# A fourth seven-product group in the gate and value half of a fused attention and SwiGLU kernel

## The chip, the cores and the metric

One core of a Trainium2 chip runs the whole kernel. The metric is the device time of one execution in microseconds (us). Every call of the chip ran the kernel before beside the kernels under test, on the same chip. A profile's span is shorter than the time by about 1.7 us.

The times of one kernel scatter by about 1% here. So, besides the times, I use the lengths of the nine chunks read from the traces.

## The reference, cut to what matters

```python
# attention over a window of 32 to both sides; q, k, v: 8 x 8 heads x 576 x 64
attn = softmax(scale * q @ k.T, masked to |i - j| <= 32) @ v
x = attn.transpose(0, 2, 1, 3).reshape(4608, 512)
# SwiGLU block, d_ff = 1536
g   = x @ w_gate
out = (g * sigmoid(g) * (x @ w_val)) @ w_out
```

## The kernel before

The 4608 tokens are worked in nine chunks of 512, numbered 0 to 8 as in the code. Each has an FFN1 part (gate and value, silu, product h) and an FFN2 part (times w_out). Attention for the next batch is threaded between the products of FFN2. It works on pairs of 64-token blocks (36 pairs, numbered through): scores (q times k), exponential, mask, product with v, normalisation to x. The pairs that the h sums below speak of are something else, pairs of h's column blocks, 0 to 5. TensorE does everything in fp16.

FFN1 of a chunk is 12 column blocks of 128. Two of them can be done "plainly", a unit of 8 matmuls of 512 columns each, or together as a "group": a 2 x 2 block product in seven instead of eight products, each of 4 matmuls of 256 columns. The seven products use three PSUM tiles. X is added to again and again, and copied or read in between:

```python
"P1": product("X", wv(0), b11, True)      # then s1: ScalarE copies X
"P2": product("Y", wv(1), b21, True)      # then c11: val half 0 = Y + s1   (VectorE)
"P5": product("Z", s1, xs[0], True)       # then p5: ScalarE copies Z
"P6": product("X", s2, xs[1], False)      # then u2: ScalarE copies X
"P7": product("X", s3, xs[2], False)      # then c22: gate = X + p5         (VectorE)
"P3": product("Z", s4, b22, False)        # then c12: val half 1 = Z + u2
"P4": product("X", wg(1), xs[3], False)   # adds onto what c22 read; then sd: silu(X)
"hm": h = silu * val                      # VectorE
```

`xs` are four differences of x (GpSimd), `s1` to `s4` here are weight sums, made once. The order is written by hand. `pg`, `pv` are the halves of plain units, `s`, `m` their silu and product; `A` and `B` are sums of h that FFN2 needs, `A` on GpSimd, `B` on VectorE. `q`, `k` issue loads:

```
pg0 pv0 s0 m0 q0 k0 q1 t0
1P1 1s1 1P2 1P5 1c11 1p5 1P6 pg1 1u2 s1 k1 check t1 t2 1P7 1P3 1c22 pv1 1c12 1sc 1P4 m1 1sd t3
... (group 2)
3P1 3P2 3s1 3P5 As3 k3 3c11 3p5 3P6 2hm q4 k4 pg3 3u2 s3 3P7 3P3 3c22 pv3 3c12 3sc 3P4 m3 3sd
pg4 3hm pv4 s4 t6 Bs0 m4 flag pg5 Bs1 pv5 s5 m5 Bs2
```

FFN2 is seven products p1 to p7 of the same kind, 12 matmuls of 256 columns each, over the PSUM tiles x and y. The start:

```python
st["p1"](); st["s1"]()                 # x; ScalarE copies it
last = wino_sums(j, 5, 6)              # VectorE: the last h sums
for f in last[:2] + list(late) + last[2:]: f()
scores(0, ps_c); scores(1); scores(2); exp(0); exp(1); exp(2)
st["p2"](); st["c11"]()                # y; VectorE: the y sum reads it
masked(0); masked(1); masked(2)
st["p6"](); st["u2"]()                 # x again
st["p5"]()                             # overwrites y: must wait for c11
```

## Time and profile before

| | before |
|---|---|
| median of 3 runs | 320.4 us (320.32 to 322.25) |
| span of the profile | 319.1 us |
| busy: TensorE, VectorE, ScalarE, GpSimd | 96, 70, 61, 55% |
| from a chunk's first plain half (pg0) to p5 of its FFN2, chunks 2 to 8 | 24.65, 24.65, 24.65, 24.64, 24.91, 23.91, 23.95 us |

The prediction shows the lines behind this. One more view: the chain of waits, which is followed back from the last instruction, at each step to what released it. Here it is from the end of FFN1 to p5 in chunk 4, in order of time (start, length, what):

```profile
172.67 0.44 PE gX_ps L484 x4
173.11 3.45 PE gv_ps L553 x16
176.56 1.31 PE x_ps L622 x12
177.87 0.81 PE s_ps L312 x48
178.68 1.42 PE y_ps L622 x12
180.10 1.31 PE x_ps L622 x12
181.41 1.31 PE y_ps L622 x12
```

Only TensorE is in it. P4 of the third group, two plain units (16 matmuls), p1, the scores of three pairs, p2, p6, p5: each starts when the one before it has been issued, and nobody is waited for.

### The profile page before, as it was taken

Reading aid. Unit: us, or ns where it says so; the run is one execution under the profiler, and the core shown is the slowest. Engines: PE = TensorE matmul, PEld = TensorE weight load, DVE = VectorE, ACT = ScalarE, POOL = GpSimd, SP = SyncE. Lnnn points to the kernel's source line nnn. Section 1 sums busy time; section 2 is a strip of 40 time slices with the busy share of each in tenths; the row PEclk is TensorE's granted clock in tenths of the full one; section 3 lists DMA queues with packets and bytes.
Section 4 is the critical chain, followed back from the end, with each engine's and each line's share of the span. In section 5 each row is a group of like instructions: output and inputs, shape, how many; then the busy total and the mean of one; then the engine's idle time right before and its main releaser. Section 6 shows DMA issues by size and latency. Waiting matters only on the chain.

```text
span 319.1 us, 8056 instructions
## 1 busy us (share of the span) xinstructions
PE 306.0 (96%) x3180; PEld 210.3 (66%) x3180; DVE 222.3 (70%) x402; ACT 196.0 (61%) x309; POOL 175.5 (55%) x199
## 2 busy tenths in 40 slices
PE   6879999999999999999999999999999999999991
PEld 3444555575877587668766877677667766777581
DVE  3854498799866788668766886876578867737750
ACT  3874569664766576757566757584757576236530
POOL 8973678539359925885489239952530439004000
PEclk9999999999999999999999999999999999999997
DMA  7999999999959997999999999999553460030012
GB/s 280 176 195 302 236 173 187 199 131 159 147 149 130 147 157 163 126 152 157 190 110 160 153 157 155 155 166 166 138 112 77 99 89 0 24 109 2 0 52 89
DMA packets 157003, 44.46 MB, mean 139 GB/s; under 512 B 137504, under 2 KB 154400, under 8 KB 156960
## 3 DMA queue, kind: packets, MB, share of 16 engines
q0 software_dynamic: 100640, 16.52, 80.2%
q1 hardware_dynamic: 56320, 27.38, 43.6%
q8 instruction: 26, 0.43, 0.6%
q14 instruction: 17, 0.14, 0.2%
HBM read 37.75 MB, written 9.44 MB: 148 GB/s over the span
## 4 chain that ended last, share of the span: by engine, by line
PE 85%; DMA 6%; DVE 4%; ACT 2%; issue 1%; SPq 0%
PE gv_ps L553 26%; PE gX_ps L484 14%; PE x_ps L622 11%; PE y_ps L622 8%; PE gZ_ps L484 6%; PE gv_ps L427 6%; DMA xT<-x 3%; PE gY_ps L484 3%; PE ob L441 3%; PE o_ps L374 3%; PE s_ps L312 2%; DMA qk_st<-in_k_dram 2%; DVE p_t L358 1%; PE z_ps L622 1%; PE xt_ps L414 1%
## 5 line engine op out<-in xcount | busy, mean ns | idle before, releaser
L558 ACT ACTIVATE ssb<-gv_ps 128x512 f16<-128x512 f32 x48 | 28.7, 597 | 36.4 <-PE gv_ps L553 36.4
L553 PE MATMUL gv_ps<-xT,wg 128*128 128x512 f16 x192 | 49.3, 379 | 0.3 <-DMA xT<-x 0.2
L553 PE MATMUL gv_ps<-xT,wv 128*128 128x512 f16 x192 | 49.3, 379 | 0.0
L562 DVE TENSOR_TENSOR hT<-ssb,gv_ps 128x512 f16<-128x512 f16 x48 | 33.0, 687 | 20.3 <-ACT ssb L558 19.7
L542 POOL TENSOR_TENSOR x_sums<-xT 128x512 f16<-128x512 f16 x14 | 16.8, 1202 | 52.5 <-issue 26.6
L318 ACT ACTIVATE p_t<-s_ps 128x1024 f16<-128x1024 f32 (+1 forms) x40 | 34.6, 924 | 13.3 <-PE s_ps L312 13.3
L590 POOL TENSOR_TENSOR s_top<-hT 128x512 f16<-128x512 f16 x16 | 18.5, 1156 | 38.4 <-DVE hT L530 31.2
L484 PEld LDWEIGHTS <-g_top 128*128 128x128 f16 x288 | 26.8, 97 | 12.1 <-ACT kept L268 3.7
L622 PEld LDWEIGHTS <-hT 128*128 128x128 f16 x288 | 27.6, 98 | 5.1
L506 DVE TENSOR_TENSOR gate<-gX_ps,kept 128x512 f32<-128x512 f32 x24 | 16.6, 690 | 19.8 <-ACT kept L268 10.0
L553 PEld LDWEIGHTS <-wv 128*128 128x128 f16 x192 | 18.8, 98 | 17.5
L622 PEld LDWEIGHTS <-s_top 128*128 128x128 f16 x288 | 27.7, 98 | 3.5 <-issue 0.2
L268 ACT ACTIVATE kept<-gX_ps 128x512 f32<-128x512 f32 x48 | 28.6, 595 | 2.1 <-ACT kept L268 2.0
L484 PE MATMUL gX_ps<-x_sums,g_top 128*128 128x256 f16 x192 | 28.9, 272 | 0.1
L223 POOL DMA_DIRECT2D tok<-in_q_dram x30 | 26.0, 865 | 4.8 <-DMA qT<-tok 1.4
L553 PEld LDWEIGHTS <-wg 128*128 128x128 f16 x192 | 18.2, 98 | 14.3 <-issue 0.3
L223 POOL DMA_DIRECT2D tok<-in_k_dram x30 | 25.9, 863 | 0.6 <-DMA wo<-in_moe_w_out_dram 0.5
L392 DVE TENSOR_TENSOR x<-o_ps,rall 128x512 f16<-128x512 f32 x36 | 24.9, 691 | 1.2
L511 ACT ACTIVATE silu<-gate 128x512 f16<-128x512 f32 x24 | 15.1, 630 | 17.0 <-DVE gate L506 17.0
L622 PE MATMUL x_ps<-w_top,s_top 128*128 128x256 f16 x192 | 23.6, 273 | 0.0
L322 DVE TENSOR_TENSOR p_t<-p_t,mask 128x1024 f16<-128x1024 f16 x32 | 21.5, 706 | 2.0 <-ACT p_t L318 1.3
L242 POOL DMA_DIRECT2D v<-in_v_dram x24 | 21.5, 916 | 0.9 <-PE s_ps L312 0.9
(114 smaller groups left out, 610.2 us busy)
## 6 DMA issues: line engine op xcount, KB each, us to landing
out_dram<-osb SPq DMA_DIRECT2D x32, 256.0 KB, 3.1
v<-v SPq DMA_DIRECT2D x12, 264.0 KB, 6.4
v<-in_v_dram POOLq DMA_DIRECT2D x24, 128.0 KB, 7.8
tok<-in_q_dram POOLq DMA_DIRECT2D x24, 128.0 KB, 6.4
tok<-in_k_dram POOLq DMA_DIRECT2D x24, 128.0 KB, 6.9
qk_st<-in_q_dram SPq DMA_DIRECT2D x4, 576.0 KB, 7.0
qk_st<-in_k_dram SPq DMA_DIRECT2D x4, 576.0 KB, 10.1
v<-in_v_dram POOLq DMA_DIRECT2D x16, 96.0 KB, 6.9
```

Source lines behind the costliest of these rows:

```text
L223: nc.gpsimd.dma_start(out=t[0:n].rearrange("p (h d) -> p h d", d=D), in_=src[b].rearrange("h s d -> s h d")[128 * m:128 * m + n])
L242: nc.gpsimd.dma_start(out=dst[:, 2 * m, :, 0:D], in_=src[128 * m - 32:128 * m + 96])
L268: nc.scalar.activation(out=o, in_=i, func=AF.Copy, bias=0.0, scale=1.0)
L318: nc.scalar.activation(out=o, in_=s, func=AF.Exp, bias=0.0, scale=1.0 / float(D) ** 0.5)
L322: nc.vector.tensor_tensor(out=flat, in0=flat, in1=mask, op=ALU.mult)
L392: nc.vector.tensor_tensor(out=x16s[m][:, a], in0=ov[:, :, :, 0:D], in1=r.unsqueeze(3).to_broadcast([128, a.stop - a.start, 4, D]), op=ALU. ...
L427: nc.tensor.matmul(out=gv[:, i, :], lhsT=w[:, g, 128 * fk:128 * fk + 128], rhs=xts[j][:, g, :], start=(g == 0), stop=(g == GS - 1))
L484: nc.tensor.matmul(out=k[name][:, n], lhsT=lhs[:, g, 128 * n:128 * n + 128], rhs=rhs[:, g, :], start=(first and n == 0 and g == 0), stop=( ...
L553: nc.tensor.matmul(out=k["gv"][:, i, :], lhsT=w[:, g, 128 * fk:128 * fk + 128], rhs=xts[j][:, g, :], start=(g == 0), stop=(g == GS - 1))
L558: nc.scalar.activation(out=k["s"], in_=k["gv"][:, 0, :], func=AF.Silu, bias=0.0, scale=1.0)
L562: "m": lambda: nc.vector.tensor_tensor(out=hts[j][:, fk, :], in0=k["s"], in1=k["gv"][:, 1, :], op=ALU.mult)}
L622: nc.tensor.matmul(out=dst[n], lhsT=lhs[:, f, 128 * n:128 * n + 128], rhs=rhs[:, f, :], start=(first and f == 0 and (split or n == 0)), st ...
```

## The change

The intent: in chunks 2 to 8 a fourth group replaces two plain units, which takes matmul columns off the engine that is busy for 96% of the span. What else is in the change makes room for that:

```diff
-    xtpool = ...bufs=3                         # SBUF for four more weight sums
+    xtpool = ...bufs=2
+    gw["more"] = t1, t2, t3, t4                # made in chunk 0, from unit 7 on
+        "h1": lambda: hm(cols(0)),             # last group: h in two token halves
+        "h0": lambda: hm(cols(1)),
-                for f in range(FKS // 2):      # FFN2: pair 4, the last group, at the end
+                for f in (0, 1, 2, 3, 5, 4):
+    """, False: """                            # the order of chunks 2 to 8
+        pg0 1P1 1s1 1P5 1P2 1p5 1P6 1c11 1u2 q0 pv0 s0 k0 q1 1P7 1P3 1c22 pg1 1c12 1sc k1 1P4 m0 1sd check
...
+        4P1 4s1 4P2 4P5 q4 k4 3hm 4c11 4p5 4P6 Bs0 4u2 pv3 s3 4P7 4P3 4c22 sc0 sc1 4c12 4sc 4P4 4h0 m3 Bs1 Bs2
+        4sd 4h1
+    """}
-        for name, fs in (("A", wino_sums(j, 0, 2, nc.gpsimd)), ("B", wino_sums(j, 2, 5))):
+        for name, fs in (("A", wino_sums(j, 0, 2 if j == 1 else 1, nc.gpsimd)),
+                         ("D", wino_sums(j, 1, 2, nc.gpsimd)), ("B", wino_sums(j, 2, split))):
-        urgent = {1: (1, 2), 2: (1, 2), 3: (0, 1)}.get(j, ())
+        urgent = {1: (1, 2), 2: (1, 2), 3: (0, 1), 4: (1,), 5: (0,)}.get(j, ())
```

`sc0`, `sc1` are the scores of the first two attention pairs, moved up from behind p1. `urgent` names pairs whose x is turned (transposed) on TensorE instead of by DMA. The two token halves also change places in the groups, so that the half that FFN2 needs first is ready first. Chunk 1 keeps the old order, but has the two xT buffers and the changed order of halves and pairs too.

More of the change, by code (lines that the diff above doesn't have):

```diff
@@ L166 @@
     xpool = fast.enter_context(tc.tile_pool(name="xp", bufs=5))
-    xtpool = fast.enter_context(tc.tile_pool(name="xt", bufs=3))
+    xtpool = fast.enter_context(tc.tile_pool(name="xt", bufs=2))
     htpool = fast.enter_context(tc.tile_pool(name="ht", bufs=1))
@@ L463, in group_weights, with token_halves, group_steps @@
         t1, t2, t3, t4 = [t.rearrange("p k (a c) -> p k a c", c=256) for t in gw["s"]]
-        return [lambda k=k, o=o, a=a, b=b, op=op:
-                nc.vector.tensor_tensor(out=o[:, k], in0=a[:, k], in1=b[:, k], op=op)
-                for o, a, b, op in ((t1, g0, g1, ALU.add), (t2, t1, v0, ALU.subtract),
-                                    (t3, v0, g0, ALU.subtract), (t4, v1, t2, ALU.subtract))
-                for k in range(2)]
-    def group_steps(j, i, xs, tiles):
-        f = 2 * i
-        x = xts[j]
-        b11, b21, b22 = x[:, 0:2, 0:256], x[:, 2:4, 0:256], x[:, 2:4, 256:512]
-        wv = lambda k: wv16[:, 2 * k:2 * k + 2, 512 * i:512 * i + 256]
-        wg = lambda k: wg16[:, 2 * k:2 * k + 2, 512 * i:512 * i + 256]
-        s1, s2, s3, s4 = [t[:, :, 256 * i:256 * i + 256] for t in gw["s"]]
+        fs = [lambda k=k, o=o, a=a, b=b, op=op:
+              nc.vector.tensor_tensor(out=o[:, k], in0=a[:, k], in1=b[:, k], op=op)
+              for o, a, b, op in ((t1, g0, g1, ALU.add), (t2, t1, v0, ALU.subtract),
+                                  (t3, v0, g0, ALU.subtract), (t4, v1, t2, ALU.subtract))
+              for k in range(2)]
+        s5 = const.tile([128, 4, 2, 256], FP16, name="g_more")
+        gw["more"] = t1, t2, t3, t4 = [s5[:, n] for n in range(4)]
+        v0, v1, g0, g1 = [w[:, 2 * k:2 * k + 2, 768:1024] for w in (wv16, wg16) for k in range(2)]
+        return fs + [lambda o=o, a=a, b=b, op=op:
+                     nc.vector.tensor_tensor(out=o, in0=a, in1=b, op=op)
+                     for o, a, b, op in ((t1, g0, g1, ALU.add), (t2, t1, v0, ALU.subtract),
+                                         (t3, v0, g0, ALU.subtract), (t4, v1, t2, ALU.subtract))]
+    def token_halves(j):
+        x = xts[j]
+        return [x[:, 2 * k:2 * k + 2, 256 * c:256 * c + 256] for k in (0, 1) for c in (1, 0)]
+    def group_steps(j, f, xs, first, tiles):
+        b11, b12, b21, b22 = token_halves(j)
+        wv = lambda k: wv16[:, 2 * k:2 * k + 2, 256 * f:256 * f + 256]
+        wg = lambda k: wg16[:, 2 * k:2 * k + 2, 256 * f:256 * f + 256]
+        s1, s2, s3, s4 = (gw["more"] if f % 2 else
+                          [t[:, :, 128 * f:128 * f + 256] for t in gw["s"]])
         k = {}
-        first = "ZX" if i == 2 else "X"
+        cols = lambda c: slice(256 - 256 * c, 512 - 256 * c)
         def product(name, lhs, rhs, first):
@@ L500, in val @@
                 k["val"] = qk16.tile([128, 2, 512], FP16, tag="qk16", name="val")
-            nc.vector.tensor_tensor(out=k["val"][:, :, 256 * c:256 * c + 256], in0=k[src],
+            nc.vector.tensor_tensor(out=k["val"][:, :, cols(c)], in0=k[src],
                                     in1=k[name], op=ALU.add)
@@ L510, in silu, with hm @@
                 k["silu"] = qk16.tile([128, 2, 512], FP16, tag="qk16", name="silu")
-            nc.scalar.activation(out=k["silu"][:, :, 256 * c:256 * c + 256], in_=k[src],
+            nc.scalar.activation(out=k["silu"][:, :, cols(c)], in_=k[src],
                                  func=AF.Silu, bias=0.0, scale=1.0)
+        def hm(c):
+            nc.vector.tensor_tensor(out=hts[j][:, 2 * f:2 * f + 2, c], in0=k["silu"][:, :, c],
+                                    in1=k["val"][:, :, c], op=ALU.mult)
         return {
@@ L516, in group_steps @@
             "s1": lambda: keep_act("s1", "X"),
-            "P2": lambda: (bank("Y"), product("Y", wv(1), b21, True)),
+            "P2": lambda: ("Y" in k or bank("Y"), product("Y", wv(1), b21, True)),
             "c11": lambda: val(0, "Y", "s1"),
@@ L529, in group_steps @@
             "sd": lambda: silu(0, "X"),
-            "hm": lambda: nc.vector.tensor_tensor(out=hts[j][:, 2 * f:2 * f + 2, :],
-                                                  in0=k["silu"], in1=k["val"], op=ALU.mult),
+            "hm": lambda: hm(slice(0, 512)),
+            "h1": lambda: hm(cols(0)),
+            "h0": lambda: hm(cols(1)),
         }
     def x_sums(j, eng):
-        x = xts[j]
-        b11, b12 = x[:, 0:2, 0:256], x[:, 0:2, 256:512]
-        b21, b22 = x[:, 2:4, 0:256], x[:, 2:4, 256:512]
+        b11, b12, b21, b22 = token_halves(j)
         t = ppool.tile([128, 4, 2, 256], FP16, tag="p2", name="x_sums", bufs=2)
@@ L624, in product @@
                                      start=(first and f == 0 and (split or n == 0)),
-                                     stop=(f == FKS // 2 - 1), skip_group_check=True)
+                                     stop=(f == 4), skip_group_check=True)
         def keep_act(name, src):
@@ L765 @@
             tw = wino_weights()
-        if u >= 8:
-            if u == 8:
-                gsum = group_weights()
-            for f in gsum[2 * (u - 8):2 * (u - 8) + 2]:
-                f()
         if u == 4:
@@ L778 @@
             place_k(transpose_qk(c16[3]), 1, 1, cast_dve)
+        if u >= 7:
+            if u == 7:
+                gsum = group_weights()
+            for f in gsum[3 * (u - 7):3 * (u - 7) + 3]:
+                f()
     dummy = const.tile([1, 1], FP32)
@@ L812 @@
     carried = [8]
-    ORDER = """
+    ORDER = {True: """
         pg0 pv0 s0 m0 q0 k0 q1 t0
@@ L819, with ffn1_grouped @@
         pg4 3hm pv4 s4 t6 Bs0 m4 flag pg5 Bs1 pv5 s5 m5 Bs2
-    """
+    """, False: """
+        pg0 1P1 1s1 1P5 1P2 1p5 1P6 1c11 1u2 q0 pv0 s0 k0 q1 1P7 1P3 1c22 pg1 1c12 1sc k1 1P4 m0 1sd check
+        2P1 2s1 2P2 2P5 1hm As0 As1 q2 2c11 2p5 2P6 2u2 pv1 s1 As2 As3 k2 2P7 2P3 2c22 pg2 2c12 2sc 2P4 m1 2sd
+        3P1 3s1 3P2 3P5 2hm Ds0 Ds1 q3 3c11 3p5 3P6 3u2 pv2 s2 3P7 3P3 3c22 Ds2 Ds3 k3 pg3 3c12 3sc 3P4 m2 3sd flag
+        4P1 4s1 4P2 4P5 q4 k4 3hm 4c11 4p5 4P6 Bs0 4u2 pv3 s3 4P7 4P3 4c22 sc0 sc1 4c12 4sc 4P4 4h0 m3 Bs1 Bs2
+        4sd 4h1
+    """}
     def table(func):
         nc.scalar.activation(out=dummy, in_=rall[0:1, 0, 0:1], func=func, bias=0.0, scale=1.0)
-    def ffn1_grouped(j):
+    def ffn1_grouped(j, scores):
         b = j + 1
@@ L832, in ffn1_grouped @@
         carried.clear()
-        if pairs:
-            pair_av(pairs[0], ps_c, False)
-        if len(pairs) > 1:
-            pair_av(pairs[1], ps_a, False)
+        for n, m in enumerate(pairs):
+            pair_av(m, ps_c if j == 1 or n < len(pairs) - 1 else ps_a, False)
         for m in pairs:
@@ L847, in ffn1_grouped @@
             steps[f"t{i}"] = tw[i + 1] if j == 1 else lambda: None
-        banks = ({"X": ps_c, "Y": ps_o, "Z": ps_o}, {"X": ps_o, "Y": ps_c, "Z": ps_o},
-                 {"X": ps_o, "Y": ps_c, "Z": ps_o})
-        for i in range(3):
-            for name, f in group_steps(j, i, xs, banks[i]).items():
-                steps[f"{i + 1}{name}"] = f
-        for i, fk in enumerate((2, 3, 6, 7, 10, 11)):
+        if j == 1:
+            groups = ((0, "X", {"X": ps_c, "Y": ps_o, "Z": ps_o}),
+                      (2, "X", {"X": ps_o, "Y": ps_c, "Z": ps_o}),
+                      (4, "ZX", {"X": ps_o, "Y": ps_c, "Z": ps_o}))
+        else:
+            groups = [(f, first, {"X": ps_o, "Y": ps_c, "Z": ps_o})
+                      for f, first in ((0, "XZ"), (2, "ZX"), (3, "XZ"), (4, "ZX"))]
+        for i, (f, first, tiles) in enumerate(groups):
+            for name, fn in group_steps(j, f, xs, first, tiles).items():
+                steps[f"{i + 1}{name}"] = fn
+        for i, fk in enumerate((2, 3, 6, 7, 10, 11) if j == 1 else (2, 3, 10, 11)):
             for name, f in unit_steps(j, fk).items():
                 steps[f"{name}{i}"] = f
-        for name, fs in (("A", wino_sums(j, 0, 2, nc.gpsimd)), ("B", wino_sums(j, 2, 5))):
+        split = 5 if j == 1 else 4
+        for name, fs in (("A", wino_sums(j, 0, 2 if j == 1 else 1, nc.gpsimd)),
+                         ("D", wino_sums(j, 1, 2, nc.gpsimd)), ("B", wino_sums(j, 2, split))):
             for i, f in enumerate(fs):
                 steps[f"{name}s{i}"] = f
+        for i in range(2):
+            steps[f"sc{i}"] = scores[i] if i < len(scores) else lambda: None
         if j == NCH - 1:
@@ L869, in ffn1_grouped, with ffn2 @@
                 steps[f"{n}{m}"] = lambda m=m, n=n: load_qk(b + 1, (m,), n) if b + 1 < B else None
-        for name in ORDER.split():
+        for name in ORDER[j == 1].split():
             steps[name]()
-        return wino_sums(j, 2, 5)[3:]
-    def ffn2(j, todo, late=()):
-        st = wino_steps(j, j == NCH - 1)
+        return [wino_sums(j, 2, split)[3]] + wino_sums(j, split, 6)
+    def ffn2(j, todo):
         n = len(todo)
         ex = {}
-        urgent = {1: (1, 2), 2: (1, 2), 3: (0, 1)}.get(j, ())
+        urgent = {1: (1, 2), 2: (1, 2), 3: (0, 1), 4: (1,), 5: (0,)}.get(j, ())
         def scores(i, pool=None):
@@ L900, in norm @@
                     pair_xt(todo[i])
+        early = [lambda: scores(0, ps_c), lambda: scores(1)]
+        late, *last = ffn1_grouped(j, [] if j == 1 else early)
+        st = wino_steps(j, j == NCH - 1)
         if n:
@@ L905, in ffn2 @@
         st["s1"]()
-        last = wino_sums(j, 5, 6)
-        for f in last[:2] + list(late) + last[2:]:
-            f()
-        scores(0, ps_c)
-        scores(1)
+        for f in last[:2] + [late] + last[2:]:
+            f()
+        if j == 1:
+            for f in early:
+                f()
         scores(2)
@@ L948 @@
     for j in range(1, NCH):
-        late = ffn1_grouped(j)
-        ffn2(j, [m for m in range(NPAIR) if (2 * m + 1) // NT == j + 1], late)
+        ffn2(j, [m for m in range(NPAIR) if (2 * m + 1) // NT == j + 1])
     fast.close()
```

## The prediction

> **What bounds the kernel now.** I number the chunks as the code does, 0 to 8; the change touches 2 to 8 and leaves chunk 1 on the old order. In the text P1 to P7 are the seven products of an FFN1 group, X, Y, Z its three PSUM tiles; a plain unit is 8 matmuls of 512 columns; p1 to p7 are the seven products of FFN2, x and y its two PSUM tiles (y is used again as z); pg0 is the first plain half of a chunk. I read the page first, then the chain of waits in order of time, then the timelines of TensorE, VectorE and ScalarE through one chunk, and last the end of chunks 7 and 8.
>
> The page: engine totals, TensorE's row of the 40 slices, the chain by engine.
>
> ```profile
> PE 306.0 (96%) x3180; PEld 210.3 (66%) x3180; DVE 222.3 (70%) x402; ACT 196.0 (61%) x309; POOL 175.5 (55%) x199
> ...
> PE   6879999999999999999999999999999999999991
> ...
> PE 85%; DMA 6%; DVE 4%; ACT 2%; issue 1%; SPq 0%
> ```
>
> TensorE is never idle between slice 4 and the last one, so only two things can move the time: matmul work taken off it, and waits put onto it. Small waits do not show as idle there, because a row's duration includes the pipeline. They show as start-to-start distances. The timeline of TensorE in chunk 4, second group:
>
> ```profile
> 163.22 0.60 PE L484 MATMUL gX_ps<-xT,wv 128*128 128x256 f16 x4
> ...
> 164.57 0.60 PE L484 MATMUL gX_ps<-x_sums,g_top 128*128 128x256 f16 x4
> 165.00 1.03 PE L553 MATMUL gv_ps<-xT,wg 128*128 128x512 f16 x4
> 165.90 0.60 PE L484 MATMUL gX_ps<-x_sums,g_top 128*128 128x256 f16 x4
> ...
> 168.07 0.60 PE L484 MATMUL gX_ps<-xT,wv 128*128 128x256 f16 x4
> ```
>
> These rows are P1, P6, a plain half, P7 and the next group's P1. The chain of waits gives 0.87 us for 8 matmuls of 256 columns and 0.86 for 4 of 512, so 0.1088 and 0.2158 us each. Nominally a group with its two plain halves needs 28 x 0.1088 + 8 x 0.2158 = 4.77; it takes 168.07 - 163.22 = 4.85. The 0.08 are P6 waiting for the copy of X after P1 and P7 waiting for the copy after P6 (165.90 - 164.57 = 1.33 where 1.30 would do). So the groups already run at the limit of their copies.
>
> The end of FFN1 in chunk 7, on VectorE, then on TensorE:
>
> ```profile
> 274.60 0.69 DVE L562 TENSOR_TENSOR hT<-ssb,gv_ps 128x512 f16<-128x512 f16 x1 [0.63 <-ACT ssb L558]
> 275.20 0.75 DVE L590 TENSOR_TENSOR s_top<-hT 128x768 f16<-128x768 f16 x2
> ...
> 277.07 0.68 DVE L651 TENSOR_TENSOR osb<-y_ps,kept 128x512 f32<-128x512 f32 x1
> ```
> ```profile
> 276.33 1.47 PE L622 MATMUL x_ps<-w_top,s_top 128*128 128x256 f16 x12
> 277.81 1.47 PE L622 MATMUL y_ps<-w_top,s_top 128*128 128x256 f16 x12
> ```
>
> 277.81 is p5. It overwrites y, so it has to wait for the sum that reads y (277.07 to 277.75), and that sum stands in VectorE's queue behind the last h sums. p6 at 276.33 has 1.31 us of work; p5 could have started at 277.64. This is the one place outside the groups where TensorE already follows VectorE, and the change works exactly there.
>
> The start of chunk 6 in the chain of waits:
>
> ```profile
> 216.62 4.42 DMA xT<-x
> 221.08 1.89 PE gv_ps L553 x8
> ```
>
> The chunk's last x (pair 27) comes by a DMA transpose and lands just before pg0. In chunk 5 it is pair 23: landed 189.00, pg0 189.13.
>
> **What the Trainium skill says.** TensorE: Matmul & The Clock Gate, section Back-to-back issue gap: for an isolated matmul 262 cycles for 256 columns and 518 for 512, at 2.4 GHz 109 and 216 ns; the trace agrees (0.1088, 0.2158), and not with the 131 ns that the section names for sustained 512-column matmuls. So work here is counted in columns. SBUF — State Buffer, section Who interferes with whom: a VectorE instruction with two SBUF inputs and a GpSimd instruction that reads SBUF exclude each other for a whole instruction. The trace agrees: in chunk 7 the silu x val product at 271.09 takes 1.18 us beside a GpSimd x sum of 270.56 to 271.71; alone it takes 0.69. VectorE: DVE Perf Modes, section The three transpose paths: 390 ns for TensorE, 1309 ns for the DMA, each for a 128x128 block. Here the DMA transpose of a pair landed after 2.4 to 6.9 us, median 3.4, and four TensorE transposes cost 0.22 us of its queue (57.10 to 57.32).
>
> **The change part by part.** (1) A fourth group replaces two plain units: 16 x 0.2158 - 28 x 0.1088 = 3.45 - 3.05 = 0.41 us less per chunk, 2.85 over seven. That is the whole certain gain.
>
> (2) The extra group brings its own 0.08 of copy waits: seven times, +0.6.
>
> (3) The last group now ends FFN1; before, four plain halves (3.45 us) lay between its P4 and p1. I follow it from P7 at T = 0, with distances from chunk 8's third group: P7 297.22, gate sum on VectorE 297.91, silu 298.63. Gate: T+0.69 to T+1.38. P4 adds onto the tile that the gate reads, so it cannot start before T+1.43. In chunks 2 to 6 P3 (0.44) and the scores of two pairs (0.57 + 0.10 for the switch) fill this: P4 at T+1.54. Chunks 7 and 8 have no scores left: P3 ends at 0.87 and TensorE waits 0.56.
>
> The first half of the silu ends at T+2.04, so the first-half h product starts at T+2.07. From there VectorE's order is: that product 0.34, the last plain unit's product 0.61, two h sums of pairs 2 and 3 0.68, the second-half product 0.45, first sum of pairs 4 and 5 0.45, its successor 0.34, three more sums 1.02, then the sum that reads y. The 0.34 and 0.45 are start-to-start distances of the four x sums of the same 128x512 size at 58.33 to 59.46 (0.45 where one needs the one before), 0.61 that of rows reading PSUM. Total 3.89: the y sum starts at T+5.96, is done at T+6.64, and p5 may start at T+6.69. TensorE alone would be there at P4 1.54 + 0.44 + p1 1.31 + scores of the third pair 0.44 + p2 1.31 + p6 1.31 = T+6.35. So p5 waits 0.34 in each of chunks 2 to 6.
>
> In chunk 7 p1 waits for the Z tile (its reader ends about T+1.98): p1 2.03, p5 could be at 5.96, so it waits 0.73, where it waited 0.17. In chunk 8, with y in two halves, the first is free at T+6.43: 0.47. Whole FFN1 from pg0 to p5: 0.86 + 3 x 4.85 + 2.71 + 6.69 = 24.81. Before it was 24.65, 24.65, 24.65, 24.64, 24.91 in chunks 2 to 6 and 23.91 and 23.95 in 7 and 8. So +0.1 to +0.2 in each of 2 to 5, -0.1 in 6, +0.9 in 7, +0.7 in 8. This already holds (1) and (2): in all +2.0.
>
> (4) h sums of pairs 0 and 1 apart: 8 GpSimd instructions of 256 instead of 4 of 512 elements. GpSimd has room (55%) and all of them end, by about 0.65 us each (my estimate from 1.15), before the last group's gate. Shorter locks, no effect on TensorE: 0.
>
> (5) Pairs 23 and 27 on TensorE: pg0 in chunks 5 and 6 comes 0.28 and 0.23 after the end of the matmuls before it, where chunk 4 has 0.08; so 0.35 to gain, against 2 x 0.22 of transposes: about 0. It is needed all the same: P5 now stands 1.3 us behind pg0 instead of 2.6, and the first x sum takes 1.15.
>
> (6) Four more weight sums in chunk 0: 1.4 us of VectorE. The backlog delays the last h product by some 0.35 and with it the third pair's scores (46.1), which take the tile that it reads. Up to +0.35.
>
> Sum of the working: +2.0 + 0.35 = about +2.4.
>
> **The rivals.** A: the gain of (1) stays and VectorE keeps pace. Then p5 starts when TensorE gets there: -0.24 in each of 2 to 5, -0.44 in 6, +0.2 in 7 and +0.1 in 8, chunk 0 unharmed: -1.1, 319.3. For it speaks that (3) rests on sums of short distances, where 0.03 each over ten instructions is the whole wait, and that the order looks arranged for this (split product, scores moved forward, pair 4 last in every product). B: p5's wait as worked out: 322.8. C: more GpSimd instructions lock out VectorE's products: the second group's product late by up to 0.6. VectorE has 0.8 to 1.1 us of idle before each gate, so this would rarely reach TensorE; if it does in half of the chunks, +1 to +2 on top, 324. D: the full gain, every wait hidden: 317.5. Against it speaks that the gate wait of chunks 7 and 8 cannot be hidden, as nothing stands between P3 and P4 there.
>
> **Range and chances.** I put more than half on B, most of the rest on A, and take the time between: 321.3 us, with 319.0 to 323.3 for 8 in 10. Two per cent are 6.4 us; D is short of it, and the sum of B and C is too. Faster 0.02, within 0.96, slower 0.02.
>
> **What would show it right or wrong.** In the changed kernel: p5 right behind the end of the y sum in chunks 2 to 7 (right), or 1.31 us after p6 with the y sum long done (wrong, A). P4 of the last group in chunks 7 and 8 about 1.43 after P7. Distance from pg0 to p5 near 24.8; 24.4 would be A. The groups at 4.85. x sums starting before pg0 in chunks 5 and 6. If TensorE's total of issue time falls by 2.9 us and the span by as much, the waits of (3) are not there and the prediction is wrong.

## The result, and the profile after

| | before | after |
|---|---|---|
| first call: median | 320.74 us | 325.15 us (4 runs, 324.65 to 326.19) |
| first call: ratio | | 1.0133, 95% interval 1.0091 to 1.0176 |
| second call: median | 321.84 us | 324.55 us (6 runs) |
| second call: ratio | | 1.0071, interval 1.0045 to 1.0098 |
| span of the first profile | 319.1 | 322.9 |

A ratio is the mean time of one kernel's fast runs over that of the other's of the same rounds, so not quite the ratio of the medians quoted. The kernel became slower by about 1%, inside the 2% that count as the same. The predicted 321.3 us, with a range to 323.3, was too low.

The lines that answer to those shown of before, from the page of the changed kernel:

```profile
PE 306.9 (95%) x3272; PEld 217.5 (67%) x3272; DVE 230.1 (71%) x429; ACT 208.1 (64%) x330; POOL 181.1 (56%) x227
...
PE 70%; DVE 13%; DMA 6%; POOL 5%; ACT 2%; issue 2%; DVEq 0%; POOLq 0%; ACTq 0%
```

TensorE's share of the chain fell from 85 to 70%, and VectorE's rose from 4 to 13%. (The 5% of GpSimd come from the loads of the first 20 us, which the chain passes through this time.) The place is plain in the chain of waits of chunk 4, at the same point as in the view of before:

```profile
177.12 0.51 PE gX_ps L495 x4
...
177.72 0.70 DVE gate L517
...
178.44 0.64 ACT silu L522
...
179.11 0.43 DVE hT L526
179.54 0.60 DVE hT L576
180.14 0.67 DVE s_top L604 x2
180.81 0.35 DVE hT L526
...
181.18 0.44 DVE s_top L604
...
181.64 0.43 DVE s_top L604
182.06 0.29 DVE ws_rest L604
...
182.65 0.42 DVE ws_rest L604
183.07 0.61 DVE osb L665
...
183.73 1.47 PE y_ps L636 x12
```

The first row is P7 of the last group, the last one p5. Between them the chain never touches TensorE: gate sum, silu, first-half h product, the last plain unit's product, two h sums, second-half product, five h sums (the cut rows hold short stretches with no known wait), the y sum, p5. P7 to p5 is 183.73 - 177.12 = 6.61 us by this view, which starts a row where the one before it ends. By the timeline, which has P7's own start, it is 6.71 (177.02 here; in chunk 3 144.54 to 151.25). The prediction's working had 6.69.

Chunk 7, TensorE's timeline and then VectorE's (the bracket gives idle time and what ended it):

```profile
274.53 0.60 PE L495 MATMUL gX_ps<-x_sums,g_top 128*128 128x256 f16 x4
274.96 0.60 PE L495 MATMUL gZ_ps<-xT,g_rest 128*128 128x256 f16 x4
275.98 0.60 PE L495 MATMUL gX_ps<-x_sums,wg 128*128 128x256 f16 x4 [0.42 <-DVE gate L517]
...
279.19 1.48 PE L636 MATMUL x_ps<-w_top,s_top 128*128 128x256 f16 x12
281.24 1.47 PE L636 MATMUL y_ps<-w_top,s_top 128*128 128x256 f16 x12 [0.56 <-DVE osb L665]
```
```profile
275.23 0.69 DVE L517 TENSOR_TENSOR gate<-gX_ps,kept 128x512 f32<-128x512 f32 x1 [0.59 <-PE gX_ps L495]
...
280.50 0.68 DVE L665 TENSOR_TENSOR osb<-y_ps,kept 128x512 f32<-128x512 f32 x1
```

P3 ends its issue at 275.40; P4 starts at 275.98, when the gate sum (275.23 to 275.92) is done. p6 is issued by 280.50; p5 starts at 281.24, when the y sum (280.50 to 281.18) is done. So two waits of 0.58 and 0.74 us lie in one chunk, and the work that the fourth group saves is 0.41.

The ledger below is worked out from TensorE's timeline. A chunk runs from its pg0 to the next one's; chunk 8 runs to the end of the last matmul, the tail from there to the end of the span. "Again" is the second call.

| chunk | before | before, again | after | after, again |
|---|---|---|---|---|
| start | 21.28 | 20.99 | 21.18 | 21.32 |
| 0 | 37.81 | 37.81 | 38.48 | 38.08 |
| 1 | 32.50 | 32.18 | 33.33 | 32.18 |
| 2 | 32.74 | 32.75 | 33.13 | 32.97 |
| 3 | 32.26 | 32.25 | 32.73 | 32.76 |
| 4 | 32.54 | 34.30 | 32.74 | 32.83 |
| 5 | 31.95 | 31.82 | 32.25 | 32.52 |
| 6 | 32.82 | 32.57 | 32.52 | 32.78 |
| 7 | 29.15 | 29.14 | 30.11 | 30.12 |
| 8 | 29.35 | 29.36 | 30.47 | 30.46 |
| tail | 6.70 | 6.73 | 5.96 | 7.38 |
| pg0 to p5 in 2 to 8 | 24.65 24.65 24.65 24.64 24.91 23.91 23.95 | 24.65 24.65 24.65 24.63 24.92 23.91 23.96 | 24.88 25.13 24.88 24.88 24.87 24.88 25.07 | 24.88 25.16 24.87 25.15 24.88 24.88 25.06 |

What repeats: 0.2 to 0.7 us more in each of chunks 2 to 5 (but for the 34.30), about 1.0 in 7, 1.1 in 8, at least 0.27 in 0. What does not repeat: the 0.83 us of chunk 1 in the first trace, which is gone in the second; the further 0.40 of chunk 0, where a matmul waited for the load of w_val (at 33.29); a single 34.30 in chunk 4 of before; the tail. Chunks 2 to 8 together went from 220.8 to 224.0 us in the first traces.

The loss of chunk 1 in the first trace was a collision, seen on VectorE and TensorE:

```profile
71.50 2.69 DVE L594 TENSOR_TENSOR ws_rest<-wo,w_top 128x768 f16<-128x768 f16 x1
```
```profile
76.66 0.60 PE L495 MATMUL gX_ps<-x_sums,wg 128*128 128x256 f16 x4 [0.99 <-DVE gate L517]
```

A weight sum that takes 0.55 us alone took 2.69 beside GpSimd's h sum of 72.25 to 73.42 (1.87 in the first trace of before), the gate sum behind it came late, and P4 waited 0.99. In the second trace of each kernel this chunk takes 32.18. It is not gone for good: in `after_one_more` (below) the same weight sum took 2.62, P4 waited 0.92 and the chunk took 33.26. So a loss of this size came in 2 of 8 traces with the change and in none of 6 without; whether the change makes it likelier is not shown.

### The profile page after: what moved, and what is told of

It is laid out like the page before. It is cut to its first block, busy times and chain, and to the rows that moved or that the text cites. A ratio compares the mean times of both kernels' runs of the same rounds, so it can differ in the third digit from the quotient of the medians.

```text
span 322.9 us, 8344 instructions
## 1 busy us (share of the span) xinstructions
PE 306.9 (95%) x3272; PEld 217.5 (67%) x3272; DVE 230.1 (71%) x429; ACT 208.1 (64%) x330; POOL 181.1 (56%) x227
## 4 chain that ended last, share of the span: by engine, by line
PE 70%; DVE 13%; DMA 6%; POOL 5%; ACT 2%; issue 2%; DVEq 0%; POOLq 0%; ACTq 0%
PE gv_ps L567 18%; PE gX_ps L495 17%; PE x_ps L636 8%; PE gZ_ps L495 7%; PE y_ps L636 7%; DMA wo<-in_moe_w_out_dram 6%; PE gY_ps L495 4%; PE o_ps L374 3%; DVE s_top L604 3%; PE ob L441 3%; DVE gate L517 2%; DVE hT L526 2%; PE s_ps L312 1%; ACT silu L522 1%; DVE osb L665 1%
## 5 line engine op out<-in xcount | busy, mean ns | idle before, releaser
L268 ACT ACTIVATE kept<-gX_ps 128x512 f32<-128x512 f32 x62 | 36.9, 595 | 10.8 <-PE gX_ps L495 10.0
L604 POOL TENSOR_TENSOR s_top<-hT 128x256 f16<-128x256 f16 (+1 forms) x30 | 21.9, 729 | 34.4 <-DVE hT L526 25.9
L567 PE MATMUL gv_ps<-xT,wg 128*128 128x512 f16 x136 | 35.0, 380 | 0.0
L567 PE MATMUL gv_ps<-xT,wv 128*128 128x512 f16 x136 | 34.9, 379 | 0.0
L526 DVE TENSOR_TENSOR hT<-silu,val 128x1024 f16<-128x1024 f16 (+1 forms) x38 | 24.4, 641 | 9.3 <-ACT silu L522 8.4
L512 DVE TENSOR_TENSOR val<-gY_ps,kept 128x512 f16<-128x512 f32 x31 | 21.2, 684 | 9.5 <-PE gY_ps L495 9.4
L495 PEld LDWEIGHTS <-wv 128*128 128x128 f16 x248 | 24.1, 98 | 4.6 <-DVE x L392 0.3
L572 ACT ACTIVATE ssb<-gv_ps 128x512 f16<-128x512 f32 x34 | 20.3, 597 | 10.2 <-PE gv_ps L567 10.2
L576 DVE TENSOR_TENSOR hT<-ssb,gv_ps 128x512 f16<-128x512 f16 x34 | 23.1, 680 | 1.7 <-ACT ssb L572 1.6
L522 ACT ACTIVATE silu<-gX_ps 128x512 f16<-128x512 f32 x31 | 18.5, 597 | 8.0 <-PE gX_ps L495 7.2
```

Of the source, the lines that this page charges most:

```text
L268: nc.scalar.activation(out=o, in_=i, func=AF.Copy, bias=0.0, scale=1.0)
L495: nc.tensor.matmul(out=k[name][:, n], lhsT=lhs[:, g, 128 * n:128 * n + 128], rhs=rhs[:, g, :], start=(first and n == 0 and g == 0), stop=( ...
L522: nc.scalar.activation(out=k["silu"][:, :, cols(c)], in_=k[src], func=AF.Silu, bias=0.0, scale=1.0)
L526: nc.vector.tensor_tensor(out=hts[j][:, 2 * f:2 * f + 2, c], in0=k["silu"][:, :, c], in1=k["val"][:, :, c], op=ALU.mult)
L567: nc.tensor.matmul(out=k["gv"][:, i, :], lhsT=w[:, g, 128 * fk:128 * fk + 128], rhs=xts[j][:, g, :], start=(g == 0), stop=(g == GS - 1))
L576: "m": lambda: nc.vector.tensor_tensor(out=hts[j][:, fk, :], in0=k["s"], in1=k["gv"][:, 1, :], op=ALU.mult)}
```

## The experiments

Theory T, the tail: with a group at the end of FFN1, VectorE's queue from the gate sum to the y sum sets p5, and the gate sum sets P4 where nothing stands between P3 and P4. Rivals: G, the shorter and more numerous GpSimd sums lock VectorE out; C, the four weight sums in chunk 0 cost it; X, the turned x; L, the loss is spread evenly over the chunks and TensorE is bound by its own work. Twelve kernels ran, in three calls. All gave the reference's result. They are the second to fourth call; the first gave the result above. The changed kernel itself ran in the first two alone, with ratios of 1.0133 and 1.0071, so a ratio from a later call has no partner in its own call.

**The changed kernel and the kernel before once more.** No edit.

> The changed kernel once more, for the noise of the ledger by chunk. 325.2 us again, ratio to before 1.013 to 1.014. Tail theory (VectorE's queue at the end of FFN1 holds up p5, and the gate sum holds up P4 in chunks 7 and 8): chunks 2 to 6 from pg0 to p5 at 24.9 us, 7 at 24.9, 8 at 25.1 as in the first trace. The loss of 0.83 us in chunk 1, whose order did not change, is either there again (then it belongs to the change) or gone (then it was the luck of two engines' meeting).

> The kernel before, as a kernel of its own: ratio 1.000 within 0.002. Chunk 1 from pg0 to pg0 32.5 us if its length is fixed by the program; 33 or more in this trace would say that it varies from run to run.

Measured: 324.55 us, ratio 1.0071 (1.0045 to 1.0098), which is less than expected, and 321.62 us, ratio 0.9986 (0.9950 to 1.0022). The ledger is above. Chunk 1 is not part of the change: 32.18 in both. Most lengths from pg0 to p5 repeat to 0.02; chunk 5 of the changed kernel has 24.88 once and 25.15 once. Chunk 4 of the kernel before took 34.30 this time, about 1.8 us more than in its first trace. The time lies at the start of chunk 5, where pg0 waited for the DMA of x:

```profile
190.28 1.02 PE L553 MATMUL gv_ps<-xT,wg 128*128 128x512 f16 x4 [1.93 <-DMA xT<-x]
```

It is the x of pair 23 (issued at 185.70, landed at 190.14), which the change turns on TensorE instead. So that part of the change takes this wait away in some executions; in how many, one such trace does not show.

**The y sum ahead of the last h sums.**

```diff
-        for f in last[:2] + [late] + last[2:]:
+        for f in last[:2]:                 # chunks 2 to 8
...
         st["c11"]()
         masked(0)
+        s3_45()
         masked(1)
         masked(2)
+        s4_23(); s4_45()
```

> The changed kernel with one reordering on VectorE in chunks 2 to 8: the sum that reads y goes ahead of the last three h sums (s3 and s4 of the last pairs, not needed before p7 and p3). Tail theory: p5 follows p6 without a wait: 0.3 us less in each of chunks 2 to 6, 0.6 in 7, 0.3 in 8, in all 2 to 2.5 us: 322.7 to 323.2. GpSimd theory (more and shorter GpSimd h sums lock out VectorE) and chunk 0 theory (four more weight sums): no change, 325.

Measured: 323.52 us, ratio 1.0044 (1.0016 to 1.0071), so about 1.0 us less than the changed kernel in the same call. pg0 to p5 fell to 24.59, 24.84, 24.58, 24.59, 24.95, 24.15 and 24.62. p5 now follows p6 without a wait in chunk 3, where the two rows are 1.31 us apart (150.58 to 151.89), and the y sum waits for TensorE instead of the other way round:

```profile
150.85 0.69 DVE L665 TENSOR_TENSOR osb<-y_ps,kept 128x512 f32<-128x512 f32 x1 [0.34 <-PE y_ps L636]
```

So p5's wait was for the y sum, as T says, and not C's. That alone would not refute G, since a VectorE slowed by GpSimd would also gain from the new order; but in the changed kernel's first trace no VectorE instruction from the gate sum to the y sum of chunks 3, 4 and 7 lasts more than its usual 0.42 or 0.69 us, so none was held up by GpSimd there. Up to p5 the seven chunks together took 2.56 us less than in the changed kernel's second trace, all that was expected. Less than half of it came home in the time: chunks 2, 4 and 6 got longer after p5 (in chunk 2 8.60 us from p5 to the next pg0, before 8.09), the seven together by 1.25. The work that the y sum had overtaken now stands ahead of the normalisation of x, and the scores of the fifth pair wait for the PSUM tile which that reads:

```profile
122.74 0.57 PE L312 MATMUL s_ps<-qT,kT 64*128 64x64 f16 x16 [0.17 <-DVE rall L391]
```

Chunk 0 took 39.76 us in this trace, 1.7 over the changed kernel's second trace. This edit does not touch it; the granted clock was 0.50 there from 22 to 25 us, and four matmuls at 23.58 took 1.91 us instead of 1.03.

**The four new weight sums in chunk 2 instead of chunk 0.**

```diff
-        if u >= 7: ... gsum[3 * (u - 7):3 * (u - 7) + 3]    # after the placing of q and k
+        if u >= 8: ... gsum[2 * (u - 8):2 * (u - 8) + 2]    # as before
+        # chunk 2: gm0 gm1 after 1c11, gm2 gm3 after 2c11
```

> The changed kernel with the eight old weight sums where they were and the four new ones moved from chunk 0 into idle stretches of VectorE in chunk 2. Backlog theory: chunk 0 gets its 0.67 us back, and chunk 1 its 0.83 too if that comes from what chunk 0 shifted: 324.5 or 323.7. If neither belongs to the weight sums: 325.

Measured: 325.35 us, ratio 1.0100 (1.0066 to 1.0134): the time did not fall, though the backlog theory expected it to. The trace shows chunk 0 at 37.82, the length that it had before. In the first trace of the changed kernel the wait of which this is the removal reads, on TensorE:

```profile
46.71 0.41 PE L312 MATMUL s_ps<-qT,kT 64*128 64x64 f16 x16 [0.37 <-DVE hT L434]
```

It is the third pair's scores waiting for the tile of chunk 0's last h product, as predicted. Of the six traces with the sums in chunk 0 four give 38.08, the others 38.48 (the load of w_val) and 39.76 (the clock). Of the eight without, six give 37.80 to 37.82. So the backlog is worth about 0.27 us. A gain of that size is lost in the times' scatter, and they do not confirm it. But 38.08 also occurs once without these sums, with another wait (`x_turned`), and so does 39.50, with the clock at 0.50 again (`both_small`, both below).

**Chunks 7 and 8 back on the old order.**

```diff
-        if j == 1:                      # and at four more places
+        if j in (1, 7, 8):
```

> The changed kernel with chunks 7 and 8 back on the old order (three groups, six plain units). Tail theory: these two chunks alone cost 0.96 + 1.11 us, because no scores are left to stand between P3 and P4, so their lengths return to 29.15 and 29.35 us and the time falls by about 2.0 us: ratio to before lower than that of the changed kernel by 0.006. Rival (the loss is spread evenly over the seven chunks, or lies in chunk 0 and 1): a fall of 2/7 of the loss, 0.7 to 1 us.

Measured: 322.95 us, ratio 1.0051 (1.0022 to 1.0080). Chunks 7 and 8 took 29.15 and 29.35 us, exactly those of before: 2.1 us less than in the changed kernel, while 2 to 6 kept 33.30, 32.71, 32.74, 32.24 and 32.51. So most of the loss that repeats sits in two chunks, and rival L falls. That rests on the ledger; the times alone would not settle it, since the ratio is 0.0082 below one of the changed kernel's and 0.0020 below the other. These two chunks still have what all chunks share of the change (two xT buffers, the order of halves and pairs), so those parts, which no run isolates, cost nothing there.

**All three repairs together.** The weight sums in chunk 2, chunks 7 and 8 on the old order, and in chunks 2 to 6 the y sum first, but with `s4_23(); s4_45()` behind `norm(1)`.

```diff
         norm(1)
+        s4_23(); s4_45()
         norm(2)
```

> The changed kernel with three repairs: new weight sums in chunk 2, chunks 7 and 8 on the old order, and in chunks 2 to 6 the y sum ahead of the last h sums, with the two s4 sums after the second x normalisation, so that the scores behind it do not wait as they did in ysum_first. Tail theory: chunk 0 37.8, chunks 2 to 6 within 0.1 us of before's lengths each or slightly under, 7 and 8 as before: ratio 0.997 to 1.001. If a fourth group could keep its 0.4 us per chunk once VectorE is out of the way, ratio 0.993.

Measured: 323.26 us, ratio 1.0044 (1.0011 to 1.0078): missed. The parts are as expected in chunks 0 (37.81), 7 (29.14) and 8 (29.36), and pg0 to p5 in 4 to 6 is 24.58, 24.59, 24.58. Yet chunk 2 took 33.19 (its new weight sums met GpSimd's x sums, pg0 to p5 25.09), and chunk 6 took 33.65, 0.8 over the first trace of before. VectorE and TensorE at the end of chunk 6:

```profile
252.67 2.94 DVE L322 TENSOR_TENSOR p_t<-p_t,mask 128x1024 f16<-128x1024 f16 x2
```
```profile
255.67 0.45 PE L374 MATMUL o_ps<-v,p_t 128*64 128x66 f16 x16 [1.02 <-DVE p_t L322]
```

Two masks of 0.69 us each took 2.94, beside GpSimd's x sums of 252.35 on. In the kernel before the first of them started 6.27 us after the y sum (244.95 to 251.22) and the x sums 6.49 after it (251.44); here they are at 6.72 and 6.40 (245.95 to 252.67 and 252.35). The repair pushed VectorE's work back by 0.45 us, behind the start of GpSimd's, and lost there more than it had won. (When GpSimd starts varies too: in the changed kernel's two traces the x sums of this place start 8.15 and 6.09 us after the y sum, the masks 5.95 and 5.96. How often the two meet is not known.) And even where it works, it brings pg0 to p5 to 24.58, against 24.65 of before in chunks 4 and 5: of the 0.41 us that the fourth group saves, 0.07 is left. A part of the rest can be read from the rows: the scores of three pairs, split in two, take 1.10 us of TensorE in chunk 3 of the changed kernel (144.97 to 146.08 less 0.44 for P3, and 146.59 to 148.33 less 1.31 for p1), in one piece 0.90 in chunk 4 of before (176.40 to 178.61 less 1.31 for p1). And the group has its 0.08 of copy waits. This version does not beat the kernel before, and none here does.

**The two small parts alone, on the kernel before.**

```diff
-        (("A", wino_sums(j, 0, 2, nc.gpsimd)), ...)        # hsums_apart
+        (("A", wino_sums(j, 0, 1, nc.gpsimd)), ("D", wino_sums(j, 1, 2, nc.gpsimd)), ...)
-        urgent = {1: (1, 2), 2: (1, 2), 3: (0, 1)}         # x_turned
+        urgent = {1: (1, 2), 2: (1, 2), 3: (0, 1), 4: (1,), 5: (0,)}
```

> The kernel before with only the GpSimd h sums of pairs 0 and 1 apart in chunks 2 to 8 (eight of 256 instead of four of 512 elements). Tail theory: no effect, ratio 1.000 within 0.002, chunk lengths as before. GpSimd lock theory: VectorE's products are held up, 0.3 us or more per chunk, ratio 1.006.

> The kernel before with only the x of pairs 23 and 27 turned on TensorE. My working: gains about as much as the eight transposes cost: chunks 4 and 5 (at whose ends they stand) within 0.15 us of before's 32.5 and 31.95, ratio 1.000 within 0.002. Rival: the DMA wait at the start of chunks 5 and 6 was worth 0.2 us each and more, ratio 0.998.

> The kernel before with both small parts of the change and without the fourth group: h sums apart on GpSimd and the x of pairs 23 and 27 on TensorE. Each alone was within noise (0.997 and 0.999). If they are worth anything together, ratio 0.995 to 0.997; if not, 1.000 within 0.003.

Measured: 320.46 us, ratio 0.9971 (0.9933 to 1.0008); 321.09, 0.9987 (0.9959 to 1.0015); 321.83, 1.0012 (0.9982 to 1.0042). None is shown to differ from before: all three intervals hold 1, though the first ratio lies outside the 0.002 that were expected, and the two that came out below 1 alone came out above it together. The ledgers agree: pg0 to p5 in chunks 2 to 5 is 24.65 in all three, in 7 23.90 or 23.91, in 8 23.95 or 23.96. With x turned, chunks 4 and 5 took 32.52 and 32.03. So rivals G and X fall as parts that cost time by themselves, on the kernel before.

**One more VectorE sum in the tail, in both kernels.**

```diff
         for f in last[:2] + [late] + last[2:]:
             f()
+        if j > 1:
+            nc.vector.tensor_tensor(out=nop_t, in0=wo16[:, 0:2, 0:256], in1=wo16[:, 0:2, 256:512], op=ALU.add)
```

> The changed kernel with one useless VectorE sum of 128x512 (0.34 us from start to start) ahead of the y sum in chunks 2 to 8. Tail theory: VectorE's queue sets p5, so pg0 to p5 grows by 0.34 us in each of the seven chunks, 2.4 us in all: about 25.21 in chunks 2, 4, 5, 6 and 7, ratio to before up by 0.007 against the changed kernel. Rival (the waits lie elsewhere, VectorE has room there): no change.

> The kernel before with the same useless sum at the same place. Tail theory: in chunks 2 to 6 the y sum waited 0.35 us for p2, so the sum fits in: 24.65 unchanged. In chunk 7, where p5 already followed the y sum, 23.91 becomes 24.25; in chunk 8 23.95 becomes 24.2. In all +0.6 us, ratio 1.002. Rival: 0.34 in every chunk, 1.007.

Measured: 328.11 us (5 runs), ratio 1.0214 (1.0185 to 1.0243), and 321.17 us, ratio 1.0016 (0.9988 to 1.0044). In the changed kernel pg0 to p5 became 25.21, 25.45, 25.21, 25.21, 25.55, 25.21 and 25.40: 0.33 us more in nearly every chunk (0.68 in chunk 6). In the kernel before it stayed at 24.66, 24.65, 24.65, 24.65 and 24.91 in chunks 2 to 6, and became 24.24 in 7 and 24.20 in 8. The y sum and p5 of chunk 4, in the kernel before and then in the changed one, both with the extra sum:

```profile
180.57 0.69 DVE L651 TENSOR_TENSOR osb<-y_ps,kept 128x512 f32<-128x512 f32 x1
181.61 1.47 PE L622 MATMUL y_ps<-w_top,s_top 128*128 128x256 f16 x12
```
```profile
184.44 0.68 DVE L665 TENSOR_TENSOR osb<-y_ps,kept 128x512 f32<-128x512 f32 x1
185.18 1.47 PE L636 MATMUL y_ps<-w_top,s_top 128*128 128x256 f16 x12 [0.46 <-DVE osb L665]
```

The same 0.34 us are free in chunks 2 to 6 of one kernel and paid in all seven chunks of the other. This is the clearest single proof that VectorE's queue sets p5 after the change, and that in chunks 2 to 6 TensorE did so before it.

**Useless matmuls between P3 and P4 in chunks 7 and 8.**

```diff
+        if j >= 7:
+            steps["sc0"] = fill_mms        # five matmuls of 256 columns into a spare tile
```

> The changed kernel with five useless matmuls of 256 columns (0.54 us of TensorE work) between P3 and P4 of the last group in chunks 7 and 8. Tail theory: P4 waits there for the gate sum in any case (0.56 us), so the work is free: chunks 7 and 8 stay at 30.11 and 30.47 us within 0.1. Rival (TensorE is bound by its own work there): +0.54 each, 1.1 us in all.

Measured: 323.80 us, ratio 1.0098 (1.0069 to 1.0127). Chunks 7 and 8 took 30.10 and 30.47, as without the filler. TensorE:

```profile
273.69 0.60 PE L495 MATMUL gZ_ps<-xT,g_rest 128*128 128x256 f16 x4
274.12 0.71 PE L849 MATMUL fill<-mask 128*128 128x256 f16 x5
274.70 0.60 PE L495 MATMUL gX_ps<-x_sums,wg 128*128 128x256 f16 x4
```

P4 starts 1.01 us after P3 with the filler, and 1.02 without (274.96 to 275.98). An extra 0.54 us of TensorE work cost nothing, so TensorE's own work does not set P4; the trace names the gate sum.

## Why the prediction was wrong, point by point

- **What bounds the kernel before: right.** TensorE, with small waits inside the groups and 0.17 us at p5 of chunk 7. The extra sum that is free in chunks 2 to 6 and shows in 7 and 8 confirms the slack that was read there.
- **The fourth group saves 0.41 us, and an old-style group still takes 4.85: right** in most cases; the second group of chunk 3 runs from 131.83 to 136.70, 4.87. In the third group of chunk 3 P7 waits 0.25 us more (25.1 instead of 24.88 to p5, also in the other trace of the changed kernel). The profile names ScalarE's copy of X; it starts 0.74 us after the copy before it, in chunk 4 0.50. Chunk 8 has the like (below). Why a copy comes late in these two groups stays open.
- **P4's gate wait in chunks 7 and 8: right.** Predicted P4 1.43 us after P7; measured 1.45.
- **p5 behind the y sum: right in place and size.** Predicted 6.69 us after P7, measured 6.71 in chunk 3 and in chunk 7. Pg0 to p5 was predicted at 24.81 and is 24.88.
- **One step that failed is the choice of the number**, "I put more than half on B, most of the rest on A, and take the time between: 321.3 us". The working itself came to about +2.4 us. The second call measured +2.7 in medians, the first +4.4. In rival A p5 starts when TensorE gets there, with about 24.4 from pg0 to p5; the traces show p5 behind the y sum and 24.87 or more in each of the seven chunks. Rival A had only two supports. One was that the short distances might be off by 0.03 each. The other was that the order looked arranged to avoid the wait. The distances held to 0.02 us over the whole chain, and a look of intent is no measurement. Averaging with A took 1.5 us off the working's 322.8. (A was also too good by its own terms: TensorE at T+6.35 gives 24.47, so -0.18 in each of chunks 2 to 5 and not -0.24. With the y sum moved ahead 24.58 was measured.)
- **The other is the size of (3), "in all +2.0".** From pg0 to p5 chunks 2 to 8 grew by 3.2 us in the first traces. Chunk 8: +0.7 predicted, +1.1 measured. By the working's own terms, with 6.43 for 6.69, its stretch should be 24.55; it took 25.07. P7 to p5 is 6.44 as predicted; the 0.5 came earlier, in the third group, which took 5.34 instead of 4.85 (297.04 to 302.38): P6 starts 0.28 late behind ScalarE's copy of X, and two small matmuls of a check take 0.21, which the kernel before pays too. Chunk 3: +0.16 predicted, +0.47 measured. The other five: 24.88 where 24.81 was predicted. Behind p5 nothing was worked out at all; chunk 2 lost up to 0.2 us there. With these the repeated part of the loss is about 3.4 us (chunks 2 to 8 3.1 in the first traces, chunk 0 0.27). The first traces' whole ledger comes to +3.8: with the 0.83 and 0.40 that did not repeat in chunks 1 and 0, less 0.84 at the start and in the tail.
- **The backlog in chunk 0: right**, up to +0.35 predicted, 0.27 in repeated traces; the further 0.40 of the first trace did not repeat.
- **Turned x and sums apart at 0: right** as far as could be measured. The x sums do start before pg0 in chunks 5 and 6 (191.40 and 191.59, 222.80 and 223.84), as foreseen. That pg0 can wait 1.93 us for the DMA of x, as in `before_again`, the working did not have.
- **Rival C (GpSimd locks VectorE out): not where it was expected, but VectorE instructions do last longer beside GpSimd's.** That went with about 1.1 us in chunk 1 of two traces (33.33 and 33.26, against 32.18) and a wait of 1.0 us in chunk 6 of `mended`. It depends on when the two engines meet. With the late DMA of x and the spells at clock 0.50 (1.7 us each) it is a third source of the scatter of about 1%, which the prediction did not work out. What share each has, and what else there is, stays open.

Left open: the exact share of each term in the 4.4 us of the first call, since the times scatter by about as much as that call and the second differ.

## What to carry to other kernels

Work taken off the busiest engine is a gain only if the queues of the other engines still reach their hand-over points in time. Follow the last dependent chain at the end of the changed stage with durations from the trace, including the engine that has 30% idle, and believe the sum when it comes out. Look also for stretches where the work that used to fill a wait has gone (no scores in the last two chunks): a saving that applies to all stages can lose in those. When a wait is repaired by moving work back, look at what the moved work meets next.

## What the Trainium skill lacked or had wrong

- TensorE: Matmul & The Clock Gate, section Back-to-back issue gap: it gives 131 ns as the sustained spacing of 512-column matmuls and says that the isolated formula over-counts there. In this kernel's long streams, with a weight load to each, the spacing is 216 ns for 512 columns and 109 for 256, as the isolated formula has it.
- SBUF — State Buffer, section Who interferes with whom: the traces agree with the exclusive lock, but the delay can be longer than the one GpSimd instruction in the way: a VectorE sum of 0.55 us took 2.69 us while one GpSimd sum of 1.17 us and two issues of loads (0.91 us each) ran beside it (2.62 us in a second trace). Whether the sum alone would have held it so long, no run here shows.
- No page that I found says what it adds when a queued VectorE instruction needs the result of the one before it. Here 128x512 fp16 sums of 0.42 us then start 0.45 us apart, and 0.34 otherwise; the tail was worked out from these.
